# A first matrix product by Strassen's scheme for three late groups of a fused retention and feed-forward kernel

## The chip, the cores and the metric

The kernel runs on one core of a Trainium2 chip. A core has a matrix engine (TensorE, PE in the profile; its weight loads are PEld), a vector engine (VectorE, DVE), a scalar engine (ScalarE, ACT), GpSimd (POOL), a queue engine that issues transfers (SyncE, SP), an on-chip memory (SBUF) and a memory of eight banks that receives matrix products (PSUM). The metric is the device time of one execution in microseconds, the median of several runs.

## The reference

```python
# B, H, S, D = 8, 8, 576, 64; d_model = H*D = 512; d_ff = 2048
scores = scale * np.matmul(q, k.transpose(0, 1, 3, 2))
gamma = 1.0 - 2.0 ** (-5.0 - np.arange(H))
rel = pos[:, None] - pos[None, :]
Dmat = np.where(rel >= 0, gamma[:, None, None] ** rel, 0.0)
x = np.matmul(scores * Dmat, v)          # then (B*S, H*D) = (4608, 512)
h = x @ w_in                             # first product,  512 -> 2048
g = np.maximum(h, 0.0) ** 2
out = g @ w_out                          # second product, 2048 -> 512
```

## The kernel before

The 4608 rows are 36 units of 128 rows, in 18 groups of two (lines 175 to 190). Units 0 to 7 are loaded as pairs into large tiles; units 8 to 35 each load k, q and v (256 KB each) through SP into a pool of five buffers (line 193), POOL casts them to fp16 (lines 422 to 440), and a transfer transposes k and q (line 448).

Retention, for each group: a short PE program of 64x64 products. From group 4 on one joint program (function `f0` in `add_ret`, line 838) does the output of a group and the scores and state sums of the next one. It wants six PSUM banks at once. DVE masks the scores (rT), makes the states (Rm, stmp, R) and writes the group's input tile xT of 512 features x 256 rows (line 802).

First product (`add_ff`, line 926): for each of eight blocks, 8 matmuls of 128 weights columns x 256 rows into one bank (line 944), ReLU on ACT into `rl` (line 952), square on ACT or, for one block of eight, on DVE (lines 962 and 964) into `gT`. That is 64 matmuls of 256 columns in a group.

Second product (`add_strassen`, line 1000, for groups 1 to 17): Strassen's scheme (Winograd's form) over a 2x2 split of rows, hidden features and output columns. Seven products p1 to p7 of 8 matmuls each stand in for eight. Four sums of blocks of g go to the tile `gS` (line 1014, DVE), four differences of w_out are made once (`wT`, line 896). Between the products, bank "a" is copied out by ACT after p1, p6 and p5 (line 1054) and goes on to accumulate, bank "c" takes p7 and then p4, and DVE adds copies to banks into the output tile (line 1064).

The order of the work is a list schedule made when the program is built (`Schedule.emit`, line 44). Each task has an engine, a modelled duration, a key, tasks that it depends on and counted resources that it takes (`ff` are the eight PSUM banks, `ld` the load buffers, `wst` the large tiles, `x` and `g` the tiles of a group). An engine that is free starts the ready task with the smallest key whose resources are there. The program that comes out has a fixed order on each engine, and a late result holds up everything behind it there. Keys are formulas around `base`, the place of a group, 32 key units a unit. Tasks marked `soft` are DVE work that GpSimd slows. `place_runs` pads with no-operations ahead of PE programs of over 200 instructions.

Of the kernel before, what the change touches and what calls it, by code (L numbers as in the profile page):

```python
# [9 lines left out]
FP32 = mybir.dt.float32  # L10
FP16 = mybir.dt.float16
ACTF = mybir.ActivationFunctionType
ALU = mybir.AluOpType


class Schedule:
# [9 lines left out]
    def add(self, eng, key, dur, fn, deps=(), acq=(), after=None, lag=0.0, soft=False, size=0):  # L26
        t = dict(size=size, pad=0, soft=soft, eng=eng, key=key, dur=dur, fn=fn, acq=acq, n=len(self.tasks), users=[], free=[], lag=lag,
                 left=len(deps), ready=0.0, lat=self.LAT[eng] if after is None else after)
        for d in deps:
            d["users"].append(t)  # L30
        self.tasks.append(t)
        return t
# [5 lines left out]
    def free(self, res, tasks):  # L38

        group = dict(res=res, left=len(tasks))  # L40
        for t in tasks:
            t["free"].append(group)

    def emit(self):
        ready = {e: [] for e in self.LAT}
# [24 lines left out]
        while True:  # L70
            for e in ready:
                if busy[e]:
                    continue
                held = []
                while ready[e]:
# [17 lines left out]
                    held.append(item)  # L93
                for item in held:
# [4 lines left out]
            while events and events[0][0] <= now + 1e-9:  # L99
                _, _, what, t = heapq.heappop(events)  # L100
                if what == "end":
# [11 lines left out]
                    for g in t["free"]:  # L113
                        push(now + t["lat"], "free", g)
# [39 lines left out]
def kernel(  # L154
# [38 lines left out]
    ld = ctx.enter_context(tc.tile_pool(name="ld", bufs=5))  # L193
    stage = ctx.enter_context(tc.tile_pool(name="stage", bufs=4))
    cast = ctx.enter_context(tc.tile_pool(name="cast", bufs=7))
    work = ctx.enter_context(tc.tile_pool(name="work", bufs=4))
    o_pool = ctx.enter_context(tc.tile_pool(name="o", bufs=4))
    x_pool = ctx.enter_context(tc.tile_pool(name="x", bufs=3))
    st_pool = ctx.enter_context(tc.tile_pool(name="st", bufs=1))
    g_pool = ctx.enter_context(tc.tile_pool(name="g", bufs=3))  # L200
    u_pool = ctx.enter_context(tc.tile_pool(name="u", bufs=2))
    r_pool = ctx.enter_context(tc.tile_pool(name="r", bufs=3))
    ps_ff = ctx.enter_context(tc.tile_pool(name="ps_ff", bufs=8, space=bass.MemoryType.PSUM))
# [7 lines left out]
    wT = [const.tile([P, NF // 2, DM // 2], FP16, name=f"wT{i}") for i in range(4)]  # L211
    junk = wT[3][:, 0:2].rearrange("p f m -> p (f m)")
# [62 lines left out]
    for hp in range(NP):  # L275
# [20 lines left out]
    PAIRED = 8  # L296
    FIRST = ["k0", "q0", "v0", "k2", "q2", "v2", "w0", "w1", "w2", "w3", "w4", "w5", "w6", "w7", "k4", "q4", "v4", "k6", "q6", "v6"]
    sched = Schedule(dict(ff=8, prS=1, prO=1, g=3, ld=5, wst=4, kq=7, v16=7, rT=2, x=3, rl=3, o=4, p1=2, u2=2, u4=2,
                          R=5, Rm=2, kqT=6))
# [11 lines left out]
    def warm():  # L311
        if not warm_ps:
            warm_ps.append(ps_ff.tile([P, 512], FP32, name="warm", tag="ff"))
        nc.tensor.matmul(warm_ps[0], lhsT=junk[:, 0:P], rhs=junk, start=True, stop=True)  # L314
# [6 lines left out]
    def dma_task(key, dur, fn, **kw):  # L321
        t = add("SP", key, dur, fn, deps=list(last_load), **kw)
# [10 lines left out]
    def add_load(u):  # L333
        kind, b, c = units[u]
        for n, (name, src) in enumerate((("k", k), ("q", q), ("v", v))):
            def fn(name=name, src=src):
                x = ld.tile([P, H, D], FP32, name=f"{name}32", tag=f"{name}32")
                tile_of[name + "32", u] = x
# [10 lines left out]
            loaded[name, u] = dma_task(0, QL if name == "q" and kind == "full" else 2.2 if (u, name) == (PAIRED, "k") else 1.2, fn, acq=("ld",) if n == 0 else ())  # L349

    def add_load_pair(name, u):
        n = "kqv".index(name)

        def fn():
            if name != "q":
                tile_of["stage", u] = stage.tile([P, 2, H, 2 * D], FP32, name="pair", tag="wst")
# [12 lines left out]
        loaded[name, u] = loaded[name, u + 1] = dma_task(0, 2.9 if not loaded else 1.41 if name == "q" else 1.81, fn, acq=("wst",) if name != "q" else (),  # L369
# [24 lines left out]
    for u in range(NU):  # L394
        if ("k", u) not in loaded:
            add_load(u)
# [7 lines left out]
    last_out1 = []  # L404
# [775 lines left out]
```

## Time and profile before

| | |
|---|---|
| Three runs, median | 289.4 us (288.22 to 289.69) |
| The profiled execution | 287.97 us, of which 286.2 us span |
| PE busy | 279.3 us |
| DVE, ACT, POOL busy | 181.9, 189.5, 84.9 us |
| Last PE work ends, last DVE work ends | about 281.3, 282.6 us |

The page gives busy times of the engines, slices of the span, the chain of work that ended last, and groups of instructions with the mean duration of one. "x28" counts instructions. Rows of the chain and of the timeline begin with start and length in us. Rows of the windows view begin with a stretch and its length, then the busy time (and count) of PE, PEld, DVE, ACT and POOL, the granted clock, the DMA share and GB/s.

### The profile page before, as it was taken

What the parts mean: (1) busy time and instruction counts of PE and PEld (TensorE: products, weight loads), DVE (VectorE), ACT (ScalarE), POOL (GpSimd) and SP (SyncE); (2) the same over time, 40 slices, a digit from 0 to 9 for tenths busy, and PEclk for the clock granted to TensorE, in tenths of its full rate; (3) what the DMA queues carried; (4) which work ended last, traced back from release to release, by engine and by line L of the source; (5) the groups of instructions that cost most, each with busy time, mean ns of one, the idle gap of its engine ahead of it and who ended that gap; (6) DMA issues with size and microseconds to landing.
All of it is one profiled execution on the core that took longest, in us unless ns stands there. A gap on an engine that the chain in (4) does not pass through costs nothing.

```text
span 286.2 us, 10573 instructions
## 1 busy us (share of the span) xinstructions
PE 279.3 (98%) x4346; PEld 236.7 (83%) x4346; DVE 181.9 (64%) x340; ACT 189.5 (66%) x365; POOL 84.9 (30%) x123
## 2 busy tenths in 40 slices
PE   8899999999999999999999999999999999999994
PEld 3578767888888898888888888888888888888883
DVE  3783489756768596449484749396779586264632
ACT  5649884678495764958583875768576764828830
POOL 6550035334325251525244233334243300000000
PEclk9999999999999999999999999999999999999999
DMA  6999999889699889889998989989897920201004
GB/s 205 291 208 207 266 293 237 168 229 169 150 226 203 200 188 219 201 210 172 229 239 180 170 188 166 228 191 207 203 191 173 197 76 2 76 28 47 2 6 141
DMA packets 119150, 49.97 MB, mean 175 GB/s; under 512 B 94784, under 2 KB 113728, under 8 KB 119104
## 3 DMA queue, kind: packets, MB, share of 16 engines
q1 hardware_dynamic: 114560, 44.84, 70.5%
q0 software_dynamic: 4224, 4.19, 8.9%
q8 instruction: 35, 0.57, 0.9%
q10 hardware_dynamic: 320, 0.26, 0.4%
q14 instruction: 11, 0.09, 0.1%
HBM read 36.70 MB, written 9.44 MB: 161 GB/s over the span
## 4 chain that ended last, share of the span: by engine, by line
PE 94%; POOL 2%; issue 2%; DVE 0%; POOLq 0%; DVEq 0%
PE ph L944 45%; PE po L1041 36%; PE psO L408 5%; PE po L984 2%; PE psS L408 2%; PE psc L408 2%; PE warm L314 1%; PE psT L489 1%; POOL mask L272 1%; POOL vx L467 0%; POOL w_in L380 0%; DVE o L1064 0%; POOL mask_full L264 0%; POOL mask_tail L264 0%; DVE p L1093 0%
## 5 line engine op out<-in xcount | busy, mean ns | idle before, releaser
L944 PE MATMUL ph<-xT,w_in 128*128 128x256 f16 x1152 | 137.7, 273 | 0.0
L944 PEld LDWEIGHTS <-w_in 128*128 128x128 f16 x1152 | 111.3, 98 | 14.7 <-issue 0.6
L952 ACT ACTIVATE rl<-ph 128x512 f16<-128x512 f32 x144 | 84.4, 587 | 54.2 <-PE ph L944 53.5
L962 ACT ACTIVATE gT<-rl 128x512 f16<-128x512 f16 x118 | 74.4, 630 | 3.6
L1041 PEld LDWEIGHTS <-gS 128*128 128x128 f16 x544 | 52.5, 98 | 6.6 <-issue 0.2
L1041 PE MATMUL po<-wT,gS 128*128 128x256 f16 x408 | 55.1, 273 | 0.0
L1041 PEld LDWEIGHTS <-gT 128*128 128x128 f16 x408 | 39.6, 98 | 5.2 <-issue 0.3
L1014 DVE TENSOR_TENSOR gS<-gT,gS 128x512 f16<-128x512 f16 (+1 forms) x51 | 33.1, 649 | 8.1 <-ACT gT L962 7.3
L1041 PE MATMUL po<-w_out,gT 128*128 128x256 f16 x272 | 36.7, 273 | 0.0
L1014 DVE TENSOR_TENSOR gS<-gT 128x1024 f16<-128x1024 f16 x34 | 27.9, 822 | 10.6 <-ACT gT L962 10.5
L1064 DVE TENSOR_TENSOR o<-po,u 128x256 f32<-128x256 f32 x33 | 14.0, 424 | 29.9 <-PE po L1041 15.1
L438 POOL TENSOR_TENSOR v<-v,vdec_full 128x512 f16<-128x512 f32 x24 | 25.9, 1079 | 21.0 <-DMA v<-in_v_dram 19.7
L422 POOL CAST kq<-k 128x512 f16<-128x512 f32 x28 | 18.8, 670 | 37.7 <-DMA k<-in_k_dram 37.5
L433 POOL CAST kq<-q 128x512 f16<-128x512 f32 x24 | 15.8, 659 | 44.8 <-DMA q<-in_q_dram 44.6
L1054 ACT COPY u<-po 128x256 f32<-128x256 f32 x34 | 12.5, 369 | 19.3 <-PE po L1041 19.1
L964 DVE TENSOR_TENSOR gT<-rl 128x512 f16<-128x512 f16 x26 | 12.9, 494 | 12.7 <-ACT rl L952 12.4
L802 DVE TENSOR_TENSOR xT<-psO,gam_full 128x512 f16<-128x512 f32 x28 | 18.0, 685 | 1.4 <-PE psO L408 1.1
L1064 DVE TENSOR_TENSOR o<-po,p 128x256 f32<-128x256 f32 x18 | 7.6, 424 | 17.1 <-ACT u L1054 8.8
L1041 PE MATMUL po<-wT,gT 128*128 128x256 f16 x136 | 17.8, 273 | 0.0
L742 DVE TENSOR_TENSOR rT<-psc,mask_full 128x512 f16<-128x512 f32 x24 | 16.5, 686 | 2.0 <-PE psc L408 0.9
L1041 PE MATMUL po<-w_out,gS 128*128 128x256 f16 x136 | 17.7, 273 | 0.0
L314 PE MATMUL warm<-wT 128*128 128x512 f16 x34 | 11.1, 460 | 1.3 <-DVE wT L213 1.3
(80 smaller groups left out, 223.0 us busy)
## 6 DMA issues: line engine op xcount, KB each, us to landing
out_dram<-o SPq DMA_DIRECT2D x32, 256.0 KB, 3.5
k<-in_k_dram SPq DMA_DIRECT2D x24, 256.0 KB, 4.1
q<-in_q_dram SPq DMA_DIRECT2D x96, 64.0 KB, 3.0
v<-in_v_dram SPq DMA_DIRECT2D x24, 256.0 KB, 3.5
pair<-in_k_dram SPq DMA_DIRECT2D x4, 512.0 KB, 7.9
pair<-in_q_dram SPq DMA_DIRECT2D x8, 256.0 KB
pair<-in_v_dram SPq DMA_DIRECT2D x4, 512.0 KB, 6.0
w_in<-in_moe_w_in_dram POOLq DMA_DIRECT2D x4, 512.0 KB, 9.1
```

The costliest lines, as they stand in the source:

```text
L408: t = nc.tensor.matmul(out_, lhsT=lhsT, rhs=rhs, start=start, stop=True, skip_group_check=True, tile_position=(64 * row, 64 * col))
L422: op(out=out_.rearrange("p (n b a d) -> p n b a d", n=2, b=2, a=2), in_=in_.rearrange("p (a n b) d -> p n b a d", n=2, a=2))
L433: nc.gpsimd.tensor_copy(out=tile_of["kq", u][:, 1].rearrange("p (t a d) -> p a t d", t=4, a=2), in_=tile_of["q32", u].rearrange("p (a t) d ...
L438: nc.gpsimd.tensor_tensor(out=t, in0=tile_of["v32", u], in1=vdec[kind].rearrange("p (h o) -> p h o", o=1).to_broadcast([P, H, D]), op=ALU. ...
L742: tile_of["masking", g] = nc.vector.tensor_tensor(out=tile_of["rT", g][:, :, a], in0=tile_of["psc", g][a].rearrange("p (s n i) -> p s n i" ...
L802: nc.vector.tensor_tensor(out=tile_of["x", g].rearrange("p n (s e i) -> p e (n s) i", s=n, e=2)[:, c], in0=y.rearrange("p (o t r) -> p o r ...
L944: nc.tensor.matmul(tile_of["ph", g, fb][:, j, :], lhsT=w_in16[:, m, fi * P:(fi + 1) * P], rhs=tile_of["x", g][:, m, :], start=(m == 0), st ...
L952: nc.scalar.activation(out=t, in_=tile_of["ph", g, fb], func=ACTF.Relu)
L962: nc.scalar.activation(out=t, in_=rl, func=ACTF.Square)
L1014: nc.vector.tensor_tensor(out=tile_of["S", g][:, k, sl], in0=in0(sl), in1=in1(sl), op=op)
L1041: nc.tensor.matmul(tile_of["pb", g, bank], lhsT=left(i), rhs=right[:, i, :], start=(start and i == 0), stop=(i == HF - 1), skip_group_chec ...
L1064: nc.vector.tensor_tensor(out=o_tile(u)[:, half * HM:(half + 1) * HM], in0=bank(x), in1=tile_of[name, g], op=ALU.add)
```

## The change

Groups 14, 15 and 16 compute their first product by the same scheme: 2x2 over rows (two units), the 512 input features and the 2048 hidden features. It is done in two halves j of the hidden features; each half has seven products of 8 matmuls of 128 columns.

- Four differences of blocks of x (T1 to T4) are made by DVE, and kept in a load buffer. Four sums of w_in (`wS`) are made once by DVE, two instructions each, each of the eight tied to the input tile of one of the groups 4 to 11; they lie in memory that pair tiles of units 0 and 4 used.
- In each half ACT copies bank "a" out as fp32 after p1, p6 and p5, into load buffers that the last five units have freed. DVE adds a copy and a bank with the ReLU in one custom instruction (three a half); ACT does the ReLU of the fourth block and then two squares of 1024 elements.
- Load buffers are one constant tile with separate tokens for k, q and v; two of its buffers also hold the v pair of unit 6. The tiles for pairs and `gS` go from four to two and a constant one.
- `h1` and `h2` limit how many halves and how many second products hold banks. From modelled time 200 on, a task that waits for a resource reserves it against later keys.
- All keys are replaced by a list `PLACES`, one number for each of the 1828 tasks in the order of their creation. Its numbers for the first third of the order follow the old one.

```diff
+RESERVE_FROM = 200.0
+PLACES = """
+1001794 1001795 1001796 1001797 1001798 1001799 1001800 1001801 1001802 1001803 1001804 1001805 1001806 1001807 1001808 1001809 1001810 1001811
...
+""".split()
     def emit(self):
+        assert len(PLACES) == len(self.tasks)
+        for t, x in zip(self.tasks, PLACES):
+            t["key"] = int(x)
...
-                    if all(self.count[r] >= t["acq"].count(r) for r in t["acq"]):
+                    if (t["inside"] or not kept.intersection(t["acq"])) and all(self.count[r] >= t["acq"].count(r) for r in t["acq"]):
...
                     held.append(item)
+                    if now >= RESERVE_FROM and t["key"] < 10 ** 5:
+                        kept.update(r for r in t["acq"] if self.count[r] < t["acq"].count(r))
...
-    ld = ctx.enter_context(tc.tile_pool(name="ld", bufs=5))
-    stage = ctx.enter_context(tc.tile_pool(name="stage", bufs=4))
+    H1, H2 = 2, 2
+    UF, OB, WST = 2, 4, 2
+    LD, KQ, V16, SB, G, KT, RB = 5, 7, 7, 0, 3, 6, 5
+    stage = ctx.enter_context(tc.tile_pool(name="stage", bufs=WST))
...
+    first_stage = const.tile([P, 2, 2, H, 2 * D], FP32, name="pair_c")
+    loads = const.tile([P, LD * 3 * H * D], FP32, name="loads")
...
+            behind_pair = T["kvx", 6] if PAIRED + 3 <= u < PAIRED + LD else []
...
-        sched.free("ld", [ck, cq, cv])
+        for name in "kqv":
+            sched.free("ld" + name, [ck, cq, cv])
...
+    def make_wS():
+        def add_wS(i, in0, in1, op, deps):
+            ts = []
+            for h in range(2 if BOTH else 1):
+                def f(h=h):
+                    sl = slice(h * HF * HM // 4, (h + 1) * HF * HM // 4)
+                    nc.vector.tensor_tensor(out=wS[i][:, :, sl], in0=in0[:, :, sl], in1=in1[:, :, sl], op=op)
+                ts.append(add("DVE", WS_KEY + 2 * i + h, 0.66, f,
+                              deps=[d[h] for d in deps] + T["kvx", 4] + T["qx", 4] + [T["x", groups[WS_GROUP + 2 * i + h][0]]] + sum((wcast[x] for x in range(4)), []), soft=True))
+            return ts
+        s1 = add_wS(0, wA[1, 0], wA[1, 1], ALU.add, [])
+        s2 = add_wS(1, wS[0], wA[0, 0], ALU.subtract, [s1])
+        s3 = add_wS(2, wA[0, 0], wA[1, 0], ALU.subtract, [])
+        s4 = add_wS(3, wA[0, 1], wS[1], ALU.subtract, [s2])
...
+    def add_ff1s(g):
...
+        for i, (out_, in0, in1) in enumerate(((T1, B12, B11), (T3, B22, B12), (T2, B22, T1), (T4, B21, T2))):
...
+        def product(j, k, x, left, right, deps, fresh, key):
+            def f():
...
+                for e in range(4):
+                    fi = 4 * j + e
+                    for m in range(HK):
+                        nc.tensor.matmul(out_[:, e], lhsT=left[:, m, fi * P:(fi + 1) * P], rhs=right()[:, m],
+                                         start=fresh and e == 0 and m == 0, stop=m == HK - 1, skip_group_check=True)
...
+        def copy_to(name, j, key, deps):
+            n = PARTS_OF.index(name)
+            at = (NU - PAIRED + (2 if n else 3) * FSET.index(g) + j + (not n)) % LD
+            def f():
+                t = tile_of[name, g, j] = loads[:, (3 * at + n) * H * D:(3 * at + n + 1) * H * D]
+                nc.scalar.copy(out=t, in_=bank(j, "a").rearrange("p e t -> p (e t)"))
...
+        def relu_sum(s, h, j, x, name, key, deps, acq=()):
+            def f():
+                new_g()
+                nc.vector._custom_dve(TENSOR_ADD_SAT, out=g_at(s, h, j), in0=bank(j, x),
+                                      in1=tile_of[name, g, j].rearrange("p (e t) -> p e t", t=P), s0=3.4028234e38, s1=0.0)
...
+        for j in js:
+            p1 = product(j, 1, "a", wA[0, 0], B11, xs, True, at(0))
...
+                c1 = copy_to("p1q", j, at(1.2), [p1])
+            p7 = product(j, 7, "c", wS[2], T3, [t[1], p1], True, at(1))
+            p6 = product(j, 6, "a", wS[1], T2, [t[2], c1, p7], False, at(2))
+            c2 = copy_to("u2q", j, at(3.2), [p6])
+            p2 = product(j, 2, "b", wA[0, 1], B21, xs + ([c1] if SEED1 else []) + [p6], not SEED1, at(3))
...
+                r11 = relu_sum(0, 0, j, "b", "p1q", at(4.5), [p2, c1] + first_g[:1], first)
...
+            p5 = product(j, 5, "a", wS[0], T1, [t[0], c2, p2], False, at(4))
+            c4 = copy_to("u4q", j, at(5.2), [p5])
+            r22 = relu_sum(1, 1, j, "c", "u4q", at(6), [p7, c4, r11])
+            p3 = product(j, 3, "a", wS[3], B22, [c4, p5], False, at(5))
+            r12 = relu_of(1, 0, j, "a", at(6.5), [p3, r11])
+            p4 = product(j, 4, "c", wA[1, 1], T4, [t[3], r22, p3], False, at(6))
+            r21 = relu_sum(0, 1, j, "c", "u2q", at(7), [p4, c2])
...
+            for s, q in ((0, square(0, j, at(8), [r11, r21])), (1, square(1, j, at(8.5), [r12, r22]))):
+                sq[s, 0, j] = sq[s, 1, j] = [q]
...
+        if strassen1(g):
+            sq = add_ff1s(g)
+            at = base + F2OFF
+            add_strassen(g, us, at, lambda s, i, h, parts: sq[s, i, h] if parts == 2 else sq[s, i, 0] + sq[s, i, 1], lambda k: at + F2ST * k)
+            return
```

More of the change, by code (lines that the diff above doesn't have):

```diff
@@ L36, in need, with free @@
         t["left"] += 1
-    def free(self, res, tasks):
-        group = dict(res=res, left=len(tasks))
+    def free(self, res, tasks, lag=0.0):
+        group = dict(res=res, left=len(tasks), lag=lag)
         for t in tasks:
@@ L113, in emit @@
                     for g in t["free"]:
-                        push(now + t["lat"], "free", g)
+                        push(now + t["lat"] + g["lag"], "free", g)
                 elif what == "dep":
@@ L313, in warm @@
             warm_ps.append(ps_ff.tile([P, 512], FP32, name="warm", tag="ff"))
+            if SB:
+                nc.tensor.matmul(ps_sb.tile([P, 512], FP32, name="seed", tag="sb"), lhsT=junk[:, 0:P], rhs=junk, start=True, stop=True)
         nc.tensor.matmul(warm_ps[0], lhsT=junk[:, 0:P], rhs=junk, start=True, stop=True)
@@ L436, in fv @@
         def fv():
[L437 removed]
+            t = tile_of["v16", u] = cast.tile([P, H, D], FP16, name="v16", tag="v16", bufs=V16)
             nc.gpsimd.tensor_tensor(
@@ L841, in f0 @@
                 emit_out1(g)
-                last_out1.append(quads[-1])
+                last = quads[-1]
                 emit_scores(g + 1)
                 emit_sums(g + 1)
-                behind(nc.tensor.nop(hint="order", nofuse=True), last_out1.pop())
+                behind(nc.tensor.nop(hint="order", nofuse=True), last)
                 emit_out2(g)
@@ L1032, in add_strassen, with product @@
+        s4 = add_sum(3, base + 4 - early, PARTS, G(0, 1), S_(1), ALU.subtract, lambda h, parts: part(0, 1)(h, parts) + (s2 if parts == 1 else [s2[h]]), eng=S4_ENG if strassen1(g) else "DVE")
         last = T["ff2"][-1:]
-        def product(k, key, bank, left, right, deps, start, stop, reads):
+        def product(k, key, bank, left, right, deps, start, stop, reads, more=()):
             for q in range(4):
@@ L1146 @@
             sched.free("R", T["Rread", g])
+    for u in range(NU - LD, NU):
+        for n in range(3):
+            holders[n, (u - PAIRED) % LD] = T["casts", u]
+    make_wS()
     for g in range(len(groups)):
```

241 lines of the change are left out of this document (188 added, 53 removed), and 54 rows, old and new, of the table PLACES.

## The prediction

> **What bounds the kernel now.** I read first the page's busy table and clock row, then the chain that ended last, the waits of PE, and last the busy time of each engine by stretch.
>
> ```profile
> span 286.2 us, 10573 instructions
> PE 279.3 (98%) x4346; PEld 236.7 (83%) x4346; DVE 181.9 (64%) x340; ACT 189.5 (66%) x365; POOL 84.9 (30%) x123
> PEclk9999999999999999999999999999999999999999
> PE 94%; POOL 2%; issue 2%; DVE 0%; POOLq 0%; DVEq 0%
> PE warm L314 <- DVE wT L213: 1.3, 1, 1.3
> PE psc L408 <- DVE kqT L506: 0.5, 1, 0.5
> PE psS L408 <- POOL vx L467: 0.3, 1, 0.3
> ```
>
> PE is busy 98% at full clock, and 94% of the chain is PE's. The three waits are all that the waits view holds for PE in the whole run, 2.1 us. So time goes down here only if PE gets less to do, and any new wait of PE is paid in full.
>
> ```profile
> core 0: us, PE busy (x) PEld busy (x) DVE busy (x) ACT busy (x) POOL busy (x), PEclk, DMA share, GB/s
> 100.00:216.97 116.97, 116.97 (x2050) 104.11 (x2050) 77.09 (x127) 79.31 (x152) 42.77 (x53) 1.00 0.94 199
> 216.97:231.40 14.43, 14.43 (x249) 12.85 (x250) 10.36 (x16) 9.90 (x19) 5.24 (x6) 1.00 0.83 172
> 231.40:245.60 14.20, 14.20 (x217) 12.62 (x218) 9.95 (x19) 9.69 (x19) 0.00 (x0) 1.00 0.07 22
> 245.60:256.70 11.10, 11.00 (x159) 9.61 (x157) 5.54 (x12) 5.92 (x12) 0.00 (x0) 1.00 0.13 49
> 256.70:270.45 13.75, 13.75 (x129) 12.32 (x127) 7.60 (x16) 11.23 (x20) 0.00 (x0) 1.00 0.11 39
> 270.45:286.20 15.75, 11.61 (x107) 10.16 (x104) 4.93 (x11) 3.60 (x10) 0.00 (x0) 0.99 0.23 67
> ```
>
> The same view for line 944 alone, the first product, 64 matmuls a group:
>
> ```profile
> 216.97:231.40 14.43, 7.82 (x65) 6.18 (x66) 1.00 0.83 172
> 231.40:237.80 6.40, 3.32 (x30) 2.82 (x31) 1.00 0.13 44
> 237.80:245.60 7.80, 4.36 (x37) 3.48 (x36) 1.00 0.02 4
> 245.60:256.70 11.10, 4.29 (x38) 3.54 (x37) 1.00 0.13 49
> ```
>
> So group 14's first product lies in the stretch from 216.97, 15's in the next, 16's from 245.60 into the stretch after it. PE is full in all of them. DVE has 4.1 and 4.2 us left in the first two, and some 5.6 and 6.1 us in the next two. DMA is nearly full until then and nearly idle after 231.4, so nothing of the changed groups waits for loads.
>
> **PE's own saving.** Group 14 to 16 each give up 64 matmuls of 256 columns for 2 halves x 7 products x 8 matmuls = 112 of 128 columns.
>
> ```profile
> 261.97 3.06 PE ph L944 x28
> 38.34 0.45 PE psT L489 x8
> L489 PEld LDWEIGHTS <-kx 128*128 128x128 f16 x32 | 2.1, 98 | 0.9 <-DVE kx L474 0.3
> 27.50 0.86 PE po L984 x4
> ```
>
> The old form costs 3.06/28 = 0.109 us each, 7.0 us a group. The new form stands in the trace as the transposes: 128 columns, each with its own 128x128 weights, 0.45 us for eight, which is one product: 14 x 0.45 = 6.3 us. So 0.69 us less a group and 2.07 us for three. Bounds: 1/8 of 7.0 is 0.87 (2.6 us in all) if cost went by columns alone; the other end is a weight load of 98 ns that no longer hides, 112 x 0.098 = 11.0 us, 4.0 us more a group. I take 0.45, the same shape with the same loads.
>
> The Trainium skill's page TensorE: Matmul & The Clock Gate, section Back-to-back issue gap, speaks against the change: a real stream of load and matmul pairs is said to run at about 81 ns for 128 columns and 131 ns for 512. The trace differs at both sizes, 56 ns for the transposes and 0.86/4 = 215 ns for 512 columns. By the page's 81 ns a group would take an estimated 9.1 us, 2.1 us more than now.
>
> **ACT.** Removed per group: 8 ReLU and 7 squares of 512. Added: 6 copies of 128x512 out of PSUM, 2 ReLU, 4 squares of 1024.
>
> ```profile
> L952 ACT ACTIVATE rl<-ph 128x512 f16<-128x512 f32 x144 | 84.4, 587 | 54.2 <-PE ph L944 53.5
> L962 ACT ACTIVATE gT<-rl 128x512 f16<-128x512 f16 x118 | 74.4, 630 | 3.6
> L991 ACT COPY o<-po 128x512 f32<-128x512 f32 x2 | 1.2, 591 | 0.0
> L1054 ACT COPY u<-po 128x256 f32<-128x256 f32 x34 | 12.5, 369 | 19.3 <-PE po L1041 19.1
> ```
>
> Removed 8 x 0.587 + 7 x 0.630 = 9.1 us. From 369 to 591 ns for 256 more columns, 512 more cost 0.44, so a square of 1024 takes about 0.63 + 0.44 = 1.07. Added 6 x 0.591 + 2 x 0.587 + 4 x 1.07 = 9.0 us. No net change; bound of the square, unseen at 1024: 0.63 to 1.26, 1.8 us less or 0.7 us more a group, beside 4.5 idle.
>
> **DVE.** Added per group: 6 sums of a PSUM bank and an fp32 copy with the ReLU in one custom instruction, and 4 differences of 128x256 fp16. Removed: one square.
>
> ```profile
> L767 DVE TENSOR_TENSOR stmp<-psS,Rm 128x512 f32<-128x512 f32 x12 | 8.3, 691 | 0.5
> L964 DVE TENSOR_TENSOR gT<-rl 128x512 f16<-128x512 f16 x26 | 12.9, 494 | 12.7 <-ACT rl L952 12.4
> L1014 DVE TENSOR_TENSOR gS<-gT,gS 128x512 f16<-128x512 f16 x34 | 18.1, 533 | 8.1 <-ACT gT L962 7.3
> L896 DVE TENSOR_TENSOR wT<-w_out 128x1024 f16<-128x1024 f16 x4 | 2.8, 688 | 5.1 <-DMA w_out<-in_moe_w_out_dram 5.1
> ```
>
> No custom instruction is in this trace; I take 0.69, from the row that also adds a PSUM bank to SBUF data. Bounds: 0.49 (all-fp16 row) and 1.38 (two passes). A difference of 256: between nothing and half of 0.533, and 0.49; I take 0.30. Sum 4.14 + 1.2 - 0.49 = +4.8 us a group, bounds +2.5 and +9.7. In the first two stretches DVE then has 10.36 + 9.95 + 9.6 = 29.9 us to do in 28.6 - 1.4 = 27.2 us: 2.7 us too many, unless second-product sums of groups 14 and 15 slip past 245.6, where 11 us are free. This is the weak point. The eight weight sums, 8 x 0.69 = 5.5 us, go one per group into DVE's 39.9 idle us between 100 and 217 (some before, in groups 4 to 6); at cost nothing, and up to 0.69 each where one stands ahead of a sum that PE awaits.
>
> **Waits that come in.** In each half, bank a goes p1, copy, p6, copy, p5, copy, p3, and bank c takes p4 only after DVE has added the copy of p5 to p7.
>
> ```profile
> 256.57 3.66 PE L944 MATMUL ph<-xT,w_in 128*128 128x256 f16 x32
> 257.70 0.60 ACT L952 ACTIVATE rl<-ph 128x512 f16<-128x512 f32 x1 [1.43 <-PE ph L944]
> ```
>
> The bank's eighth matmul issues out at 256.57 + 0.87 = 257.44, and ACT starts at 257.70, so a copy sends the bank back 0.26 + 0.59 = 0.85 us after PE left it. p7 and p2 hide 0.45 of the first two. The third has nothing of its own half before p3. p4 then needs 0.69 + 0.1 of DVE less 0.45 of p3. Bare, that is 0.4 + 0.4 + 0.85 + 0.34 = 2.0 us a half, 12 us for six halves. What hides it is other PE work put between: the other half, 6.1 us of second product for each group (56 x 0.109), and the first product of group 17. Queued behind a late copy on ACT is the next square, and behind that the sums of the second product. I take 0.3 us that shows in all.
>
> **Edits costed at nothing.** The sums use load buffers whose last readers are the casts for units 31 to 35; two load buffers share bytes with the pair tile of unit 6:
>
> ```profile
> 209.90 1.36 POOL L438 TENSOR_TENSOR v<-v,vdec_full 128x512 f16<-128x512 f32 x1
> 224.43 1.36 POOL L438 TENSOR_TENSOR v<-v,vdec_tail 128x512 f16<-128x512 f32 x1 [0.68 <-DMA v<-in_v_dram]
> 231.39 3.16 PE ph L944 x28
> 44.59 1.04 POOL L467 TENSOR_TENSOR vx<-pair,vdec_pair 128x512 f16<-128x512 f32 x1 [0.61 <-DMA pair<-in_v_dram]
> 60.03 0.44 SPq L344 DMA_DIRECT2D k<-in_k_dram  x1
> ```
>
> Unit 33's cast ends at 211.3, before group 14's product at 216.97; unit 35's at 225.8, before group 15's at 231.39: 5.6 us of cover each, lost only if the products move that far forward. The pair cast ends at 45.6 and unit 11's load, the first that waits for it, is issued at 60.03. SP issues the same transfers in the same dependence, so its queue gains nothing to wait for; the separate k, q and v tokens are given back by the same three casts. Two buffers instead of four for the feature sums suffice as long as one group's last p3 comes before the next group's first sum, as in the old order. The order after the first third is a new list: it moves joint programs, products and DVE tasks of all later groups. Between 100 and 217 PE has no idle time to win, so this can only lose; bounds 0 and, say, one 0.69 DVE instruction exposed per group, 8 us. I take 0, since DVE is 66% and ACT 68% busy there.
>
> Sum: -2.07 + 0.3 = **-1.8 us**. The profiled execution took 287.97 us (span 286.2 and 1.8 around it), so 286.2. It lies 1.4 under the median of the three runs, 289.4; against that, 287.6.
>
> **Rivals.**
>
> *DVE's backlog swallows it.* For: 29.9 us of work in 27.2. Against: sums are wanted late, and DVE is half idle after 245.6. If half the excess reaches PE, 2.07 - 1.35 = 0.7 us stays: 288.7; if all of it, 290.0.
>
> *Slower: bank a and bank c in turn stop PE.* One mechanism, p5, copy, sum, p4 in six halves: 0.85 + 0.34 = 1.2 us bare each. Its place is between p5 and p4. It decides from 2.07/6 = 0.35 us a half. With half of it exposed, 3.6 - 2.07 = +1.5: 290.9; bare, +5.1: 294.5. For: three banks a half of the eight, while a joint program wants six, leave little other PE work that can be started there. Against: the second product works its banks in the same turn, and PE never waits for it.
>
> *Load-bound matmuls.* With 98 ns a matmul, +12 us: 301; with the loads half hidden, 295.4. Against: the transposes' row. By the 81 ns of the Trainium skill's page TensorE: Matmul & The Clock Gate, section Back-to-back issue gap, it would be an estimated +6.2 us.
>
> *The new order costs time in the middle.* Two of nine groups expose 0.69 us twice each, 2.8 us: 290.4. It is also the way in which the change would not do what it says, the saving made late and lost early.
>
> **How the numbers follow.** Forecast 0.45; backlog 0.27; bank turns 0.20; load-bound 0.03; order 0.05. 0.5% is 1.4 us, about what a measurement of this kernel can tell from no change, so the forecast passes it by little: 0.44 faster; 0.28 same, nearly all of the backlog case and a part of the others; 0.28 slower. The likeliest case alone runs from 286.2 (lowest run 288.22 less 2.07) to 288.2. The range goes up to 290.8, which leaves out the bare bank turns and the load-bound case: 286.2 to 290.8.
>
> **What would show it.** Right: 112 matmuls of 128 columns in each of three groups, eight in 0.45 us; PE's work some 2 us less; waits of PE on ACT copies or DVE sums under 0.5 us in all; custom sums at 0.69. Wrong: matmuls near 80 or 98 ns; PE idle in the windows of groups 14 to 16 behind the copy of p5 or the ReLU sum; DVE over 95% there with PE idle; PE waits between 100 and 217.

## The result, and the profile after

| | before | after |
|---|---|---|
| Median of six runs each | 288.75 us (288.22 to 289.69) | 285.79 us (285.17 to 287.10) |
| Ratio, with its 95% interval | | 0.9896 [0.9867, 0.9926] |
| The profiled execution | 287.97 us, span 286.2 | 285.26 us, span 283.5 |
| PE busy | 279.3 us in 4346 matmuls | 276.7 us in 4490 |
| DVE, ACT, POOL busy | 181.9, 189.5, 84.9 us | 194.7, 190.6, 86.4 us |

The change makes the kernel 1.0% faster. The forecast of 287.6 us had the sign and the mechanism, but the time lies 0.4 us below the low end of its range, 286.2. Two executions of `copy_after_p5_twice`, further below, were slow (354.85 us at a granted clock of 0.754, which is also the one traced, and 290.84 us), and its ratio leaves them out. First the page of the changed kernel: busy times, clock and the summary of the chain.

```profile
span 283.5 us, 10916 instructions
...
PE 276.7 (98%) x4490; PEld 236.3 (83%) x4490; DVE 194.7 (69%) x371; ACT 190.6 (67%) x360; POOL 86.4 (30%) x123
...
PEclk9999999999999999999999999999999999999999
...
PE 95%; POOL 2%; issue 2%; DVE 0%; POOLq 0%
```

PE is still the bound: 98% busy, 95% of the chain, full clock. Its waits in the whole run, all that the waits view of the changed kernel holds (total, times, longest, in us):

```profile
PE warm L408 <- DVE wT L289: 1.3, 1, 1.3
PE psT L581 <- DVE qx L564: 0.5, 1, 0.5
PE psc L499 <- DVE kqT L598: 0.5, 1, 0.5
PE psS L499 <- POOL vx L559: 0.3, 1, 0.3
```

None of them belongs to the groups 14 to 16. The wait on `qx` is new here. It comes back in a second trace of the changed kernel (0.4 us in `after_again` below), but not in an equivalent order (`late_p3`). Next, the chain of the changed kernel, rows of start, length and work:

```profile
224.04 3.57 PE ph L1069 x64
...
237.10 2.68 PE ph L1069 x48
...
268.94 10.93 PE po L1324 x100
```

64 matmuls of 128 columns, each with weights of its own, take 3.57/64 = 0.0558 us apiece, and 48 take 2.68/48 = 0.0558. With that price the change removes 192 x 0.109 = 20.9 us of PE work and adds 336 x 0.0558 = 18.7: 2.2 us less. The ends of the two programs show the same amount. The last DVE instruction in the timeline of before, and of the changed kernel:

```profile
282.14 0.42 DVE L1064 TENSOR_TENSOR o<-po,p 128x256 f32<-128x256 f32 x1
```

```profile
279.90 0.42 DVE L1347 TENSOR_TENSOR o<-po,p 128x256 f32<-128x256 f32 x1
```

It starts 2.24 us earlier. (The last PE work of before ends at 282.06 us in this trace, not at about 281.3 as the table ahead of the prediction has it.) The span is shorter by 2.76 us (286.25 to 283.49 in the trace), so 0.5 us more went somewhere behind the last computation. That part is taken up below.

The windows of before and of the changed kernel (stretch, length, then PE, PEld, DVE, ACT, POOL busy, the clock, DMA share, GB/s) show where the added DVE work went:

```profile
200.00:220.00 20.00, 20.00 (x400) 17.69 (x399) 15.39 (x24) 12.70 (x25) 6.26 (x8) 1.00 0.90 194
220.00:240.00 20.00, 20.00 (x388) 17.73 (x386) 14.68 (x26) 12.08 (x24) 4.01 (x4) 1.00 0.53 114
240.00:260.00 20.00, 19.90 (x240) 17.60 (x239) 9.12 (x19) 13.28 (x26) 0.00 (x0) 1.00 0.15 54
```

```profile
200.00:220.00 20.00, 20.00 (x393) 17.72 (x392) 16.10 (x29) 13.99 (x27) 7.20 (x9) 1.00 1.16 203
220.00:240.00 20.00, 20.00 (x400) 18.87 (x392) 18.30 (x37) 13.82 (x24) 3.57 (x4) 1.00 0.51 113
240.00:260.00 20.00, 19.90 (x306) 18.39 (x305) 13.79 (x26) 14.02 (x24) 0.00 (x0) 1.00 0.08 29
```

DVE rises to 18.30 of 20 us, 92%, while PE stays full, and to 13.79 in the stretch behind it, where there was room. The same view by the stretches of the prediction, 14.43 and 14.20 us taken together, again before and after:

```profile
200.00:216.97 16.97, 16.97 (x372) 14.98 (x371) 12.50 (x19) 10.30 (x20) 5.04 (x6) 1.00 0.93 200
216.97:245.60 28.63, 28.63 (x465) 25.47 (x466) 20.30 (x34) 19.59 (x38) 5.24 (x6) 1.00 0.45 97
```

```profile
200.00:216.97 16.97, 16.97 (x273) 15.08 (x271) 15.21 (x27) 12.34 (x24) 6.58 (x8) 1.00 1.18 188
216.97:245.60 28.63, 28.53 (x626) 26.38 (x624) 23.55 (x47) 18.18 (x32) 4.19 (x5) 1.00 0.46 110
```

DVE takes on 2.7 us ahead of 216.97 and 3.3 us from there to 245.6. The costs of the new instructions, from the costliest groups by shape (busy, mean ns, idle before and its releaser):

```profile
L1103 DVE CUSTOM_DVE_ANT_0 gT<-ph,loads 128x512 f16<-128x512 f32 x18 | 12.0, 686 | 4.0 <-PE ph L1069 3.5 <-ACT loads L1082 0.5
...
L1082 ACT COPY loads<-ph 128x512 f32<-128x512 f32 x18 | 10.2, 586 | 3.1 <-PE ph L1069 2.4 <-issue 0.5
...
L1117 ACT ACTIVATE gT<-gT 128x1024 f16<-128x1024 f16 x12 | 12.2, 1055 | 0.1
...
L1054 DVE TENSOR_TENSOR loads<-xT 128x256 f16<-128x256 f16 x3 | 0.9, 290 | 0.1
```

Last, the turns of bank "a" in group 14, from the timeline of the changed kernel (start, length, instruction, and in brackets the idle time ahead of it with its releaser):

```profile
225.66 0.61 PE L1069 MATMUL ph<-xT,w_in 128*128 128x128 f16 x8
...
225.86 0.58 ACT L1082 COPY loads<-ph 128x512 f32<-128x512 f32 x1 [0.40 <-PE ph L1069]
...
226.11 0.61 PE L1069 MATMUL ph<-loads,pair_c 128*128 128x128 f16 x8
...
226.55 0.61 PE L1069 MATMUL ph<-xT,w_in 128*128 128x128 f16 x8
226.75 0.58 ACT L1082 COPY loads<-ph 128x512 f32<-128x512 f32 x1 [0.31 <-PE ph L1069]
...
227.00 0.61 PE L1069 MATMUL ph<-loads,pair_c 128*128 128x128 f16 x8
...
227.34 1.28 DVE L1103 CUSTOM_DVE_ANT_0 gT<-ph,loads 128x512 f16<-128x512 f32 x2
...
227.45 0.38 PE L1324 MATMUL po<-wT,gS 128*128 128x256 f16 x2
...
227.65 1.25 ACT L1082 COPY loads<-ph 128x512 f32<-128x512 f32 x2 [0.31 <-PE ph L1069]
227.67 0.61 PE L1069 MATMUL ph<-loads,pair_c 128*128 128x128 f16 x8
...
228.11 0.38 PE L1324 MATMUL po<-wT,gS 128*128 128x256 f16 x2
```

A row of eight matmuls reads 0.61 us, because the end of the last one is modelled (219 ns each); the next run starts 0.45 later, at 226.11 and 226.55. Products of the two halves alternate, and when both are turning a bank, two matmuls of the second product (L1324) lie between. So ACT copies one bank while PE fills another, without a gap.

### The profile page after: what moved, and what is told of

Read it like the earlier page. It is cut to its first block, busy times and chain, and to the rows that moved or that the text cites. A ratio compares the mean times of both kernels' runs of the same rounds, so it can differ in the third digit from the quotient of the medians.

```text
span 283.5 us, 10916 instructions
## 1 busy us (share of the span) xinstructions
PE 276.7 (98%) x4490; PEld 236.3 (83%) x4490; DVE 194.7 (69%) x371; ACT 190.6 (67%) x360; POOL 86.4 (30%) x123
## 4 chain that ended last, share of the span: by engine, by line
PE 95%; POOL 2%; issue 2%; DVE 0%; POOLq 0%
PE po L1324 37%; PE ph L1226 37%; PE ph L1069 7%; PE psO L499 5%; PE po L1267 2%; PE psc L499 2%; PE psS L499 2%; PE warm L408 1%; PE psT L581 1%; POOL mask L348 1%; POOL vx L559 0%; POOL w_in L475 0%; POOL mask_full L340 0%; POOL mask_tail L340 0%; DVE o L1347 0%
## 5 line engine op out<-in xcount | busy, mean ns | idle before, releaser
L1226 PE MATMUL ph<-xT,w_in 128*128 128x256 f16 x960 | 117.5, 273 | 0.0
L1226 PEld LDWEIGHTS <-w_in 128*128 128x128 f16 x960 | 93.0, 98 | 12.4 <-issue 0.6
L1234 ACT ACTIVATE rl<-ph 128x512 f16<-128x512 f32 x120 | 70.3, 590 | 42.2 <-PE ph L1226 41.5
L1244 ACT ACTIVATE gT<-rl 128x512 f16<-128x512 f16 x101 | 63.5, 630 | 2.7
L1324 PEld LDWEIGHTS <-gS 128*128 128x128 f16 x544 | 51.4, 98 | 6.7 <-issue 0.4
L1324 PE MATMUL po<-wT,gS 128*128 128x256 f16 x408 | 55.2, 273 | 0.0
L1324 PEld LDWEIGHTS <-gT 128*128 128x128 f16 x408 | 39.3, 98 | 5.2 <-issue 0.4
L1297 DVE TENSOR_TENSOR gS<-gT,gS 128x512 f16<-128x512 f16 (+1 forms) x51 | 30.6, 607 | 10.2 <-ACT gT L1244 9.6
L1324 PE MATMUL po<-w_out,gT 128*128 128x256 f16 x272 | 37.6, 273 | 0.0
L529 POOL TENSOR_TENSOR v<-loads,vdec_full 128x512 f16<-128x512 f32 x24 | 25.9, 1079 | 32.2 <-DMA loads<-in_v_dram 22.9
L513 POOL CAST kq<-loads 128x512 f16<-128x512 f32 x32 | 22.4, 698 | 37.9 <-DMA loads<-in_k_dram 29.0
L524 POOL CAST kq<-loads 128x512 f16<-128x512 f32 x24 | 16.9, 702 | 37.3 <-DMA loads<-in_q_dram 37.3
L1337 ACT COPY u<-po 128x256 f32<-128x256 f32 x34 | 12.4, 369 | 16.6 <-PE po L1324 16.4
L1324 PE MATMUL po<-wT,gT 128*128 128x256 f16 x136 | 19.0, 273 | 0.0
L1324 PE MATMUL po<-w_out,gS 128*128 128x256 f16 x136 | 18.7, 273 | 0.0
L1103 DVE CUSTOM_DVE_ANT_0 gT<-ph,loads 128x512 f16<-128x512 f32 x18 | 12.0, 686 | 4.0 <-PE ph L1069 3.5
L1246 DVE TENSOR_TENSOR gT<-rl 128x512 f16<-128x512 f16 x19 | 10.2, 541 | 6.5 <-ACT rl L1234 6.3
L608 DVE TENSOR_TENSOR R<-stmp,dec 128x512 f16<-128x512 f32 (+1 forms) x18 | 12.7, 703 | 0.4
```

The costliest lines, as they stand in the source:

```text
L513: op(out=out_.rearrange("p (n b a d) -> p n b a d", n=2, b=2, a=2), in_=in_.rearrange("p (a n b) d -> p n b a d", n=2, a=2))
L524: nc.gpsimd.tensor_copy(out=tile_of["kq", u][:, 1].rearrange("p (t a d) -> p a t d", t=4, a=2), in_=tile_of["q32", u].rearrange("p (a t) d ...
L529: nc.gpsimd.tensor_tensor(out=t, in0=tile_of["v32", u], in1=vdec[kind].rearrange("p (h o) -> p h o", o=1).to_broadcast([P, H, D]), op=ALU. ...
L1226: nc.tensor.matmul(tile_of["ph", g, fb][:, j, :], lhsT=w_in16[:, m, fi * P:(fi + 1) * P], rhs=tile_of["x", g][:, m, :], start=(m == 0), st ...
L1234: nc.scalar.activation(out=t, in_=tile_of["ph", g, fb], func=ACTF.Relu)
L1244: nc.scalar.activation(out=t, in_=rl, func=ACTF.Square)
```

## The experiments

Each batch had the kernel before beside it on the same chip: medians 288.02 us (25 runs), 288.18 (24) and 288.15 (23) for the three batches. Ratios are to these.

### Which part carries the gain: buffers, list, scheme

**The buffers and tokens alone.** Old keys, no reservation, plain first product everywhere.

```diff
-RESERVE_FROM = 200.0
-PLACES = """
...
+RESERVE_FROM = 1e9
...
-        assert len(PLACES) == len(self.tasks)
-        for t, x in zip(self.tasks, PLACES):
-            t["key"] = int(x)
...
-    FSET = (14, 15, 16)
+    FSET = ()
```

> The changed kernel without its three visible parts: no group by Strassen in the first product, no list of places (the old keys) and no reservation. What is left is the new buffers, the separate tokens for loads and the eight weight sums, which nobody reads here. Theory (the saving is PE's own work, the rest is free): the time of the kernel before, 288.75 us within 0.5, span near 286.2. Rival (the rebuilt buffers or the order of creation give a part of the gain): 287.5 us or less.

Measured: 288.09 us, ratio 0.9999 [0.9972, 1.0027]. The constant load tile, the separate tokens, the smaller tile pools and the eight weight sums cost nothing that can be measured and bring nothing.

**The list alone.** The groups 14 to 16 keep the plain product; its tasks get places spread over those of the products that they replace.

```diff
 PLACES = """
...
-    FSET = (14, 15, 16)
+    FSET = ()
```

> The changed kernel with its list of places and its reservation, but groups 14 to 16 with the plain first product, whose tasks take places spread over those of the Strassen tasks. Theory (Strassen's matmuls are the gain): PE has 2.1 to 2.2 us more to do than in the changed kernel and next to nothing else changes, so 287.9 to 288.3 us; the trace shows about 2.1 us more of PE work. Rival (the new order is worth something by itself): 287.0 us or less, with the last PE work under 1.5 us later than in the changed kernel.

Measured: 288.53 us, ratio 1.0016 [0.9995, 1.0038]. The list gains nothing by itself. The kernel lies 3.2 us above an equivalent of the changed one in the same batch (`late_p3` below, 285.28), where only the 2.2 us of PE work were taken back; it has waits of its own. From the waits view of its trace:

```profile
PE psc L505 <- DMA kqT<-kq: 1.0, 1, 1.0
PE psT L587 <- DVE qx L570: 1.0, 1, 1.0
PE ph L1232 <- DVE xT L901: 0.5, 1, 0.5
```

The last stands in its chain at 234.3 us, behind a row of ACT and DVE steps from 227.3 on: an order made for one set of instructions is not good for another. The places of the plain tasks are a choice of this experiment, so it bounds what the list brings alone, no more.

**The scheme alone.** Strassen for the three groups, with the old formulas as keys.

```diff
-PLACES = """
...
-        assert len(PLACES) == len(self.tasks)
-        for t, x in zip(self.tasks, PLACES):
-            t["key"] = int(x)
```

> The changed kernel with Strassen in groups 14 to 16 and the reservation, but the old keys in place of the list. Theory (bank turns would stop PE, and only the list puts other work between): PE waits behind copies, ReLU sums and full banks for 4 to 5 us between 200 and 245 us, so about 290 to 291 us, slower than before. Rival (turns hide in any order): 286.5 us or less.

Measured: 287.40 us, ratio 0.9974 [0.9955, 0.9993]. The expected loss did not come: the kernel is faster than before, but by 0.6 us where PE has 2.2 us less to do. Waits and windows of its trace:

```profile
PE po L1264 <- ACT u L1277: 0.5, 1, 0.5
...
PE ph L1009 <- ACT loads L1022: 0.4, 1, 0.4
```

```profile
200.00:220.00 20.00, 19.69 (x410) 17.37 (x408) 15.28 (x29) 12.77 (x25) 6.24 (x9) 1.00 0.89 196
220.00:240.00 20.00, 19.69 (x504) 18.22 (x504) 17.06 (x33) 12.62 (x22) 3.42 (x5) 1.00 0.48 110
```

Here PE does stop for a copy of bank "a" (L1022): once, for 0.40 us, at 220.21 us. That is a bank turn of the prediction, and the only wait on one in the six halves. The other wait is not one. It stands at 276.29 us, in the last group's second product, 16 us behind the last product of the new scheme, and the copy (L1277) started as soon as PE had filled its bank, with no copy of a bank "a" of the scheme near it. With the list both waits are gone. In the traced execution they account for what is missing: its span is 1.29 us shorter than that of before (284.96 against 286.25), which is 2.2 less 0.9. That execution was the quickest of ten, 0.7 us under the median of 287.40; where the others lost that, no trace shows. Neither part has the gain by itself (0.9974 and 1.0016); together they give 0.9896.

### Is PE the bound in the three groups?

One matmul of 128 columns more in each of the 42 products (a term of one block is added twice).

```diff
                         nc.tensor.matmul(out_[:, e], lhsT=left[:, m, fi * P:(fi + 1) * P], rhs=right()[:, m],
                                          start=fresh and e == 0 and m == 0, stop=m == HK - 1, skip_group_check=True)
+                        if e == 1 and m == 0:
+                            nc.tensor.matmul(out_[:, e], lhsT=left[:, m, fi * P:(fi + 1) * P], rhs=right()[:, m],
+                                             start=False, stop=False, skip_group_check=True)
```

> The changed kernel with a ninth matmul of 128 columns in each of the 42 products (it adds one term twice, so the output is another). PE gets 42 x 0.056 = 2.35 us more to do in the three groups and nothing else changes. Theory (PE is the bound there, each ns of it is paid): 2.2 to 2.4 us more than the changed kernel beside it. Rival (PE has hidden slack there, waits that the longer products cover): 1.5 us or less.

And the changed kernel once more beside it, unedited:

> The changed kernel as it is, with more runs beside the kernel before. Theory (2.16 us of PE work, and the 0.46 us of the stores was scatter, since moving p3 back cost nothing): the ratio comes out nearer to 0.9925 (2.16 of 288) than to 0.9896. Rival (something else of about 0.8 us was gained): 0.9896 or less again.

Measured: 288.06 us, ratio 1.0000 [0.9979, 1.0021], against 285.88, ratio 0.9908 [0.9880, 0.9936], for the unedited one. 2.18 us for 42 x 0.0558 = 2.34 us of work: PE's time is paid nearly in full, in the groups where the change saved it. The ratio of the unedited kernel does not decide between its own two expectations: the interval holds both 0.9925 and 0.9896. The gain against before is 2.30 us in this batch and 2.96 in the first.

### How much room do the bank turns have?

The copy after p5 issued twice in each half, 0.59 us later for whoever waits:

```diff
-                nc.scalar.copy(out=t, in_=bank(j, "a").rearrange("p e t -> p (e t)"))
+                for _ in range(2 if name == "u4q" else 1):
+                    nc.scalar.copy(out=t, in_=bank(j, "a").rearrange("p e t -> p (e t)"))
```

> The changed kernel with ACT's copy of bank a after p5 issued twice, which writes the same data again. Each of the six halves gets 0.59 us later at the turn that has no product of its own half to hide it. Theory (other PE work stands between p5 and p3, with room to spare): 0.5 us or less. Rival (the turns have no room): 6 x 0.59 = 3.5 us.

Measured: 286.89 us (286.79 without the two longest), ratio 0.9948 [0.9928, 0.9967]: 0.9 to 1.0 us above the changed kernel of the same batch, of 6 x 0.59 = 3.5 us added. That is more than the 0.5 us expected and far from the rival's 3.5. Then all three copies of a half, the same loop without the condition:

```diff
+                for _ in range(2):
+                    nc.scalar.copy(out=t, in_=bank(j, "a").rearrange("p e t -> p (e t)"))
```

> All 18 copies of bank a out of PSUM issued twice: 18 x 0.58 = 10.4 us more of ACT, and each of the three returns of bank a in a half 0.58 us later. The copy after p5 alone, twice, cost 1.0 us. Theory (the turns of the banks are hidden with about 0.4 us of room each): 2.5 to 5 us above the changed kernel, ratio 0.999 to 1.007, with PE waits on ACT in the groups 14 to 16. Rival (only the turn behind p5 is tight, since p7 and p2 cover the two others): 1.0 to 1.5 us above, ratio 0.994 to 0.996.

Measured: 290.03 us, ratio 1.0059 [1.0037, 1.0082], 4.5 us above the quickest form of the changed kernel in that batch (`after_sp_nops`, 285.50). Timeline of its trace at the same place in group 14, and its first wait of PE:

```profile
225.38 5.63 ACT L1083 COPY loads<-ph 128x512 f32<-128x512 f32 x10
...
225.56 0.61 PE L1069 MATMUL ph<-xT,w_in 128*128 128x128 f16 x8
...
226.65 0.61 PE L1069 MATMUL ph<-loads,pair_c 128*128 128x128 f16 x8 [0.48 <-ACT loads L1083]
...
228.85 0.61 PE L1069 MATMUL ph<-loads,pair_c 128*128 128x128 f16 x8 [0.28 <-ACT loads L1083]
```

```profile
PE ph L1069 <- ACT loads L1083: 2.3, 6, 0.5
```

ACT now copies without a break for 5.63 us, and PE, which went from product to product every 0.45 us, stops 0.48 us ahead of one. So the mechanism of the slower rival exists in this kernel; the order gives it room for one copy, not for two. All three copies cost more than four times the one: the turns after p1 and p6 have no more room than that after p5, or ACT as a whole is too full for them. The runs do not tell these apart.

### How much room does DVE have?

The sum on p7 (4.1 us of DVE in all), then all 18 sums (12.4 us), issued twice:

```diff
-                nc.vector._custom_dve(TENSOR_ADD_SAT, out=g_at(s, h, j), in0=bank(j, x),
...
+                for _ in range(2 if (s, h) == (1, 1) else 1):
+                    nc.vector._custom_dve(TENSOR_ADD_SAT, out=g_at(s, h, j), in0=bank(j, x),
...
```

For all 18 the loop stands without its condition.

> The changed kernel with the ReLU sum ahead of p4 (bank c, block 22) issued twice, same data again. DVE gets 6 x 0.69 = 4.1 us more work between 220 and 260 us, where it was busy 32.1 of 40. Theory (DVE has 8 us left there and sums are wanted late): 0.5 us or less. Rival (DVE's queue is the next bound, sums come just in time): 2 to 4 us.

> All 18 ReLU sums of the changed kernel issued twice, the same result written again: 18 x 0.69 = 12.4 us more of DVE. The first and third sum of a half stand between a product and the next user of its bank. Between 200 and 240 us DVE was 36.4 of 40 us busy, so two groups' 8.3 us more exceed the room by 4.7 us. Theory (DVE's room, not its share, is what keeps the backlog from PE): 3 to 6 us above the changed kernel, ratio 1.000 to 1.010, with PE waits on DVE and DVE at 100% in 200 to 240. Rival (sums are wanted late anyway): under 1.5 us above it, ratio below 0.995.

Measured: 286.55 us, ratio 0.9926 [0.9899, 0.9954], 0.7 us above the changed kernel of its batch for the one, with intervals that overlap; 290.79 us, ratio 1.0082 [1.0058, 1.0107], 5.3 us above `after_sp_nops` for the other. The trace of the first holds one wait of PE on such a sum, 0.2 us. The trace of the second, windows and the first row of PE's waits:

```profile
220.00:240.00 20.00, 18.04 (x374) 15.82 (x363) 18.69 (x34) 12.11 (x20) 2.46 (x4) 1.00 0.42 77
240.00:260.00 20.00, 18.49 (x302) 16.98 (x300) 18.64 (x36) 11.99 (x21) 0.00 (x0) 1.00 0.15 55
```

```profile
PE ph L1069 <- DVE gT L1104: 2.4, 6, 0.7
```

The DVE backlog is real too: PE waits six times for a bank that a sum still reads, as often as there are halves. It does so at 93% busy, not at the 100% that was expected: DVE has idle moments, and PE stops all the same, since what it waits for is one sum and not DVE's total. 4.1 us more cost little and 12.4 us more cost 5.3, so the changed kernel stands a few us of DVE work from this rival.

### The half microsecond at the end

**A later start of the last group's p3**, by places for its four tasks behind all others, was to delay the first store of that group.

```diff
 PLACES = """
...
-1497 1514 1428 1485
+1800 1801 1802 1803
```

> The changed kernel, but the last group's product p3 stands behind the last products of group 16 again, as in the kernel before, so the first quarter of its output is stored about 2 to 3 us later, next to the others. Theory (the last stores left earlier, and that is the 0.46 us by which span minus last DVE work went down): 0.3 to 0.5 us more than the changed kernel, and about 3.6 us from the last DVE work to the end. Rival (the landing of the last stores scatters from run to run): no change, within 0.2 us.

Measured: 285.28 us, ratio 0.9897 [0.9865, 0.9929]. In the trace that store still leaves at 275.65 us (275.93 in the changed kernel): PE's order at the end is the same in both traces. The list schedule starts the ready task with the smallest key, so a late place does not hold back a task that nothing ready stands ahead of; whether that was so here no run shows. The edit did not do what it was for, so it says nothing on the stores. It stands as another run of the changed kernel.

The traces tell more. In before, the last store is issued at 282.59 us and lands at 284.79; in the changed kernel at 280.35 and 282.58. That is 2.20 and 2.23 us, the same. From there to the end of the span it takes 1.46 and 0.91 us. In this closing sequence SP waits for every store, all engines drain, and POOL clears the semaphores. Read from the instruction records of SP in each trace:

```text
kernel             SP instructions   pause ahead of the 336th   last landing to end
before                   340            0.36 us, closing            1.46 us
frame_plain              339            0.37 us, closing            1.46 us
strassen_formula         339            0.39 us, closing            1.45 us
list_plain               338            0.39 us, closing            0.90 us
after                    338            0.39 us, closing            0.91 us
before_sp_nops           362            before the closing          0.97 us
after_sp_nops            360            before the closing          0.91 us
```

In all twelve traces of kernels with 338 to 340 of them, SP stands still for 0.36 to 0.41 us ahead of the 336th. With 340 and 339 that is SP's drain, for which POOL and then all engines wait. With 338 it is the instruction after that drain, and POOL's own drain and clearing go on meanwhile; all nine traces with 338 close in 0.90 to 1.00 us. The place in the count is what these pauses share: in all fourteen traces SP stands still as well ahead of its 80th instruction (0.45 to 0.48 us) and its 208th (0.37 to 0.39 us), each 128 from the next, whatever instruction that is. Two experiments moved it away:

```diff
     def store(u, o, lo=0, hi=DM, engs=(nc.sync, nc.sync)):
         kind, b, c = units[u]
+        if u == 20:
+            for _ in range(22):
+                nc.sync.nop(hint="order", nofuse=True)
```

> The kernel of before with 22 no-operations more on SP, issued in the middle of the run where SP has nothing due. In every trace so far SP stands still for 0.36 to 0.41 us right ahead of its 336th recorded instruction; the kernel of before has 340 in all, so that stands in the closing sequence. Theory (the 0.5 us at the end that the prediction did not foresee comes from SP's instruction count, 338 in the changed kernel): with 22 more, the pause moves to an earlier instruction, while the last stores are not due, and the time from the last landing to the end falls from 1.46 to 0.9 us or below; 0.5 us less than the kernel before, ratio about 0.998. Rival (the order list or the layout of the end causes it): the closing time stays at 1.46 us, ratio 1.000.

> The changed kernel with the same 22 no-operations on SP. Theory: its pause of 0.39 us, of which part is hidden behind POOL's closing instructions, leaves the closing sequence too: 0.1 to 0.4 us less than the changed kernel, about 285.5, ratio 0.988 to 0.990. Rival: no change in the time from the last landing to the end (0.9 us).

Measured: the kernel before with the no-operations closes in 0.97 us instead of 1.46 (0.9 or below was expected); its 336th SP instruction is now a store at 259.2 us. Its time is 287.79 us, ratio 0.9988 [0.9969, 1.0008], 0.36 us less, too little to be told from none by the clock alone. The changed kernel with them closes in 0.91 us as it did without, which was a miss: its pause had been hidden wholly, not in part. Its time, 285.50 us, ratio 0.9921 [0.9895, 0.9948], is no different from the changed kernel's. So the trace shows that the number of SP instructions sets whether the pause lies in the open, and that the changed kernel has two fewer: one goes with the buffers and tokens (339 in `frame_plain` and `strassen_formula`, which still close in 1.46 and 1.45 us), the other with the list (338, with the scheme or without it), and it is the second that hides the pause. What SP does in the pause no run shows.

## Why the prediction was right and wrong

**PE's own saving: right.** 0.45 us for a product of eight (3.57/64 x 8 = 0.446) as taken from the transposes; 2.07 forecast, 2.2 by the chain's rows and 2.24 at the last DVE instruction; the difference is 0.446 rounded up to 0.45 in 42 products. The rival of load-bound matmuls is settled by the chain's row of 64: 55.8 ns apiece, though the weight loads are listed at 98 ns each. The 81 ns of the Trainium skill's page TensorE: Matmul & The Clock Gate, section Back-to-back issue gap, does not hold in this kernel.

**The prices on ACT and DVE: right; one count was not.** Taken and measured: 0.69 and 0.686 for the sum, 0.591 and 0.586 for the copy, 1.07 and 1.055 for the square of 1024, 0.30 and 0.29 for a difference of 256 between tiles of x. Differences that read a load buffer were longer (0.41 on average). By the groups of DVE, 12.0 us of sums, 4.3 of differences and 5.7 of weight sums came, and 2.7 of squares went (seven, where three were counted, so that 17 and not 21 left ACT, whose busy time rose by 1.1 us): 19.3 where 3 x 4.8 + 5.5 = 19.9 was summed. DVE's busy time rose by 12.8 only. Of the 6.5 us between, 4.3 are in the 85 sums of blocks of g (34 + 34 + 17), which took 56.7 us and not 61.0; why, no run shows, and the rest was not located.

**The DVE backlog (0.27): it did not come, but not by the escape that was named.** The prediction said that 29.9 us do not go into 27.2 (it takes 1.4 us off the two stretches without saying why) unless second-product sums slip past 245.6. They did not: ten of these sums of blocks of g touch the stretch from 216.97 to 245.6 before and after, and behind it, until 270.45, 13 do in place of 12 (6.5 us and 6.3). DVE is busy for 23.55 us in that stretch, not for 29.9. More of its work lies ahead, 15.21 us and not 12.50 between 200 and 216.97, the four differences of group 14 among it. The products of group 14 start at 223.0 and no longer at 216.97, and two ReLU sums of group 15 end behind 245.6. From 240 to 260, where DVE is busy 4.7 us longer than before, its ReLU sums take 7.4 us and its sums of blocks of g 3.5 (4.0 before). So the step that put the 29.9 us into that stretch took the places of the work from the old order. The doubled sums show that the rival was near all the same.

**The bank turns (0.20): hidden, as forecast.** In the changed kernel no wait of PE on them is left, so the 0.3 us that the forecast allowed did not show. With the old keys one shows, 0.4 us of the bare 12. The room is narrow: a copy more at each turn costs 4.5 us.

**Edits at nothing: right for the buffers** (`frame_plain`, 0.9999). **The new order: the step that failed.** The prediction says that "PE has no idle time to win, so this can only lose", takes 0 and gives a bound on one side only. The argument looked at PE's idle time between 100 and 217 us and left out what lies behind PE's last matmul; of SP it asked what its queue waits for, not how many instructions it holds. There the list left SP one instruction fewer than `frame_plain` has, and the closing sequence went from 1.46 to 0.91 us in the traces: 0.55 us won where only a loss was thought possible. That is more than the 0.41 us by which the time lies below the range. With the scheme in place the list is worth 2.1 us in its batch (287.40 against 285.28 for `late_p3`). By the clock alone the 0.5 us is not told from none (`before_sp_nops`: 0.36 us, with an interval that holds none).

**The base.** 289.4 us was the median of three runs; of six it is 288.75, and in the three later batches 288.02 to 288.18. That is 0.65 us of the 1.8 us between 287.6 and 285.79. The closing sequence is 0.55, the waits that did not come 0.3, the saving at 2.24 and not 2.07 another 0.17: 1.67 in all, and the other 0.14 is within the scatter of runs.

**The range's low end.** It was "lowest run 288.22 less 2.07", the value taken. The prediction's own bound for the same term was 2.6; with it the low end would have been 285.6 and held the time. So the range carried the bounds of the losses and not that of the gain.

## What to carry to other kernels

Where one engine is 98% busy at full clock, count its instructions and take their price from a row of the same shape: that term came out within a tenth. What stands between the count and the clock is the order, so test scheme and order apart: here each alone brought a fourth of the gain or nothing. A stretch that looks too full by the old order says little about a new one, which can move work out of it on both sides. And read the trace behind the last computation as well; an edit that only reorders can win or lose half a microsecond there.

## What the runs showed of the hardware

- SP stands still for 0.36 to 0.41 us ahead of its 336th recorded instruction in all twelve traces whose closing sequence falls there, and for 0.37 to 0.48 us ahead of its 80th and 208th in all fourteen. Where the pause falls ahead of a drain that other engines wait for, the closing sequence takes 0.5 us longer; 22 no-operations earlier in the queue take it away (1.46 to 0.97 us).
- 64 matmuls of 128 columns in a row, each with its own 128x128 weights, run at 55.8 ns, half of the 109 ns for 256 columns: the weight loads, listed at 98 ns, stay hidden over the whole run.
- PE waits for a transposing transfer somewhere between 112 and 118 us in three of the fourteen traces (0.7 us in `frame_plain`, 1.0 in `list_plain`, 0.6 in `all_sums_twice`) and not in those of before and of the changed kernel. Whether that goes with the kernel or with the single execution, one trace each does not show; it can make up to 1 us of difference between two traces.
